# The first product of the last two blocks by seven half-size products per step, with sums of w_in kept in old q/k tiles and three output buffers

## The chip, the cores and the metric

The kernel runs on one core of a Trainium2 chip. The time is the device time of one execution, in microseconds (us); 204.36 is the median of three runs of the kernel before (204.35 to 204.37). One more execution was taken by the profiler. Engines are named as the profile does: PE multiplies matrices (PEld loads its weights, beside it), DVE and ACT work on vectors, POOL and SP issue transfers. SBUF is the working memory of 128 partitions, PSUM the memory of eight banks that PE writes into; a bank holds 128 x 512 fp32 numbers.

## The reference

An attention layer is followed by a two-layer network without bias.

```python
scores = scale * (q @ k.T) + bias            # 4 batches, 8 heads, 768 tokens, head width 64
scores = where(is_global | is_local, scores, -1e9)   # 8 global keys, 96 local keys
a = softmax(scores)
x = (a @ v) as [3072 tokens, 512]
h = x @ w_in                                 # [3072, 2048]   the "first product"
r = maximum(h, 0)
g = r * r
out = g @ w_out                              # [3072, 512]    the "second product"
```

All inputs and the output are fp32; the kernel multiplies in bf16 and accumulates in fp32.

## The kernel before

**Attention** runs over 24 tiles of 128 tokens (j = 0 to 23; six per batch). For each, q, k and v are loaded by POOL's queue (L267, L270), converted to bf16 on the way, into a ring of tiles `qk_ring` (L197); the first tile's q and k come as fp32 into two tiles called plain. q and k are transposed on PE for the first six tiles (words tr and T) and by a DMA on SP's queue from then on (T, L487). Scores (sc), exp on ACT, a multiplication by a mask (mul), the product with v (pv) and the division by the sum (norm) give x, which is transposed into xT, on PE for the first eight tiles, then by a DMA on SP's queue (xT, L795).

**The network** works on 12 blocks of 256 tokens, two tiles each, and splits the hidden width of 2048 into 8 steps of 256. A step of the first product (`emit_s1`, L816 and on, matmul in L826) has 8 matmuls: two halves c of the hidden columns by four parts of the 512 inputs, each with weights of 128x128 from w_in and 256 moving columns of xT. They fill one whole PSUM bank, the tile hT. ACT takes the relu out of it into hr, fp32 (L849), and ACT or DVE squares hr into the bf16 tile hs (L865, L867).

**The second product** of block 0 is plain (L1104). For blocks 1 to 11 it is done by `seven` (L913 and on): the matrices are cut into 2 by 2 parts, and seven products p1 to p7 of half size take the place of eight. Sums of the parts of hs are made by DVE (hsum, L932; words sum), sums of w_out once (w_sum; words wsum), PE adds up the products in two half-filled banks x and y (L975), copies of partial results (part, L390) are taken on ACT or DVE, and `fin` adds these to later products into the output tile o (L1051), of which there are four (NO = 4). SP stores it (L1073).

**Order.** `Plan.run` (L38) emits the operations in the order of the list ORDER (L54 on, 1106 words), which is written into the kernel. A word names an operation, its block or tile and its step: s1.10.3 is step 3 of the first product of block 10, s2.9.p6.1 the second half of product p6 of block 9, @A or @V the engine. Each engine works through its own instructions in the order in which the list has them. The list lets first products run ahead of second ones: before s2.9.p1 there stand s1.10.0 and s1.10.3. PSUM's eight banks are two for `acc` and six, tag "g", for everything else. The waits between engines are put in by the framework, from the tiles that instructions read and write.

Of the kernel before, what the change touches and what calls it, by code (L numbers as in the profile page):

```python
# [54 lines left out]
tr.0.0 T.0.0@A ld.k.1 tr.1.0 ld.q.1 tr.1.1 ld.v.0 bias.0.0 ld.k.2 T.1.1@V tr.0.1 T.1.0@A T.0.1@V sc.0.0 bias.1.0  # L55
sc.1.0 exp.0.1.0 tr.1.2 exp.0.0.0 ld.q.2 exp.1.1.0 bias.1.1 pv.0.0 norm.0.0 exp.1.0.0 ld.q.3 sc.1.1 ld.v.1 T.1.2@A
exp.1.1.1 tr.0.2 gk.1 tr.0.3 T.0.2@V pv.0.1 ld.k.3 exp.1.0.1 bias.2.0 sc.2.0 norm.0.1 pv.1.0 ld.v.2 tr.1.3 norm.1.0
T.0.3@A exp.2.1.0 pv.1.1 exp.2.0.0 T.1.3@V ld.win.0.1 ld.win.0.0 norm.1.1 trx.0 gv.1 ld.win.6.0 xT.0@V bias.2.1 sc.2.1
exp.2.0.1 gk.2 pv.2.0 norm.2.0 exp.2.1.1 trx.1 sc.3.0 sc.3.1 xT.1@V pv.2.1 ld.v.3 exp.3.0.0 exp.3.0.1 E0.0 s1.0.0
exp.3.1.0 s1.0.0#2 s1.0.0#3 s1.0.0#4 ld.win.3.0 s1.0.6 norm.2.1 mul.3.0.0 gv.2 ld.k.4 mul.3.1.0 trx.2 mul.3.0.1  # L60
exp.3.1.1 ld.q.4 mul.3.1.1 pv.3.0 pv.3.1 norm.3.0 norm.3.1 relu.0.0 xT.2@A relu.0.6 ld.win.4.0 s1.0.3 s1.0.3#2 gk.3
sq.0.0@A ones.6 trx.3 tr.1.4 T.1.4@A relu.0.3 ld.win.1.0 tr.0.4 xT.3@V sq.0.6@A s1.1.0 T.0.4@V s1.1.6 ld.q.5 ld.k.5
relu.1.0 s1.1.4 sq.0.3@V sq.1.0@V relu.1.6 ld.win.2.1 ld.win.2.0 gv.3 s1.0.1 sq.1.6@V relu.1.4 s1.0.1#2 sc.4.0
sq.1.4@A relu.0.1 tr.0.5 ld.wout.0 exp.4.0.0 s1.1.3 sq.0.1@V sc.4.1 T.0.5@A s1.0.4 mul.4.0.0 exp.4.1.0 ld.win.5.0 E0.1
ld.v.4 s1.0.2 relu.1.3 sq.1.3@A exp.4.1.1 gk.4 s1.1.2 ld.win.7.0 mul.4.1.0 s2.0.0.0 tr.1.5 relu.1.2 s2.0.0.1 exp.4.0.1
s1.0.2#2 s1.0.2#3 sq.1.2@V ld.v.5 T.1.5@A mul.4.0.1 s1.0.2#4 relu.0.4 ld.wout.2 s1.0.5 ld.wout.1 relu.0.2 sq.0.4@V
pv.4.0 s1.1.7 sq.0.2@A mul.4.1.1 norm.4.0 relu.0.5 relu.1.7 pv.4.1 sc.5.0 norm.4.1 sc.5.1 ld.wout.5 exp.5.0.0 sq.0.5@V
s1.1.5 sq.1.7@A gv.4 mul.5.0.0 exp.5.1.0 exp.5.1.1 s1.0.7 exp.5.0.1 ld.wout.3 relu.1.5 mul.5.1.0 trx.4 xT.4@V
mul.5.0.1 s2.0.1.0 mul.5.1.1 pv.5.0 ld.wout.4 norm.5.0 relu.0.7 s1.1.1 ld.wout.7 pv.5.1 norm.5.1 s2.0.1.1 s2.0.2.1
s2.0.2.0 s2.0.3.0 sq.1.5@V trx.5 s2.0.4.0 s2.0.5.0 s2.0.3.1 s2.0.4.1 wsum.0.0 relu.1.1 ld.wout.6 load.6 load.7 xT.5@V  # L70
sq.1.1@V s2.0.5.1 sq.0.7@A s1.2.0 relu.2.0 sq.2.0@A wsum.0.1 wsum.2.0 s2.0.6.0 sum.1.0 sum.1.1 s2.0.7.0 s1.2.3
relu.2.3 wsum.2.1 gate.8 o.0.0@A wsum.1.0 s2.0.6.1 s2.0.7.1 s1.2.6 s2.1.p1.0 T.6 relu.2.6 T.7 s1.2.7 sq.2.3@A sq.2.6@A
s1.2.5 load.8 s2.1.p1.1 sum.1.3 part.1.p1@A s1.2.4 wsum.1.1 relu.2.5 o.0.1@A s2.1.p6.0 relu.2.7 s1.2.2 st.0.1 sq.2.5@A
st.0.0 s2.1.p2.0 wsum.3.0 relu.2.2 s2.1.p2.1 s2.1.p6.1 sq.2.7@A o.1.p2 sum.1.2 relu.2.4 sc.6.0 part.1.p6@A s2.1.p5.0
exp.6.0.0 sq.2.4@V wsum.3.1 s2.1.p5.1 exp.6.1.0 sc.7.0 mul.6.0.0 sc.7.1 s2.1.p7.0 exp.7.0.0 T.8 s2.1.p7.1 gate.9
sq.2.2@A mul.6.1.0 exp.7.1.1 part.1.p7@V s1.2.1 exp.7.1.0 mul.7.0.0 pv.6.0 mul.7.1.1 o.1.p5 exp.7.0.1 norm.6.0 pv.6.1
relu.2.1 mul.7.1.0 mul.7.0.1 s2.1.p4.0 s2.1.p4.1 sq.2.1@A o.1.p4@A s2.1.p3.0 s2.1.p3.1 norm.6.1 load.9 st.1.1 pv.7.1
pv.7.0 o.1.p3 s2.2.p1.0 st.1.0 norm.7.0 trx.6 norm.7.1 s2.2.p1.1 s2.2.p2.0 xT.6@A trx.7 T.9 gk.7 sum.2.0 s2.2.p2.1
xT.7@V sc.8.0 sc.8.1 s1.3.0 s1.3.3 gate.10 sum.2.1 exp.8.0.0 exp.8.1.0 s1.3.7 part.2.p1@A relu.3.0 load.10 exp.8.0.1
gv.7 mul.8.0.0 sum.2.2 sq.3.0@A s1.3.2 exp.8.1.1 mul.8.0.1 s2.2.p6.0 mul.8.1.0 relu.3.7 s2.2.p6.1 relu.3.2 mul.8.1.1  # L80
load.11 sq.3.7@V o.2.p2 pv.8.1 pv.8.0 relu.3.3 s1.3.5 part.2.p6@A norm.8.0 s2.2.p5.0 s2.2.p7.0 sq.3.3@A sq.3.2@A gk.8
sum.2.3 relu.3.5 s2.2.p5.1 sc.9.0 norm.8.1 gv.8 xT.8 exp.9.1.0 mul.9.1.0 sc.9.1 T.10 load.12 sq.3.5@V exp.9.0.0
exp.9.1.1 mul.9.0.0 exp.9.0.1 s2.2.p7.1 s1.3.1 part.2.p7@V mul.9.1.1 s1.3.6 o.2.p5 relu.3.1 relu.3.6 s1.3.4 sq.3.1@A
pv.9.0 mul.9.0.1 s2.2.p4.0 norm.9.0 pv.9.1 norm.9.1 gk.9 s2.2.p4.1 relu.3.4 sq.3.4@A o.2.p4@A s2.2.p3.0 s2.2.p3.1
sq.3.6@A xT.9 s2.3.p1.0 load.13 o.2.p3 s2.3.p1.1 sum.3.0 s2.3.p2.0 part.3.p1@A T.11 sum.3.1 s2.3.p2.1 sum.3.2 sc.10.0
exp.10.1.0 sc.10.1 s2.3.p6.0 s2.3.p6.1 o.3.p2 exp.10.0.0 gv.9 mul.10.1.0 s2.3.p5.0 s2.3.p5.1 part.3.p6@V exp.10.0.1
mul.10.0.0 exp.10.1.1 s2.3.p7.0 mul.10.0.1 load.14 gk.10 mul.10.1.1 s2.3.p7.1 part.3.p7@A pv.10.0 pv.10.1 s1.4.0
norm.10.0 s1.4.7 norm.10.1 relu.4.0 sc.11.0 sc.11.1 s1.4.4 T.12 relu.4.7 s1.4.3 sq.4.0@V exp.11.0.0 o.3.p5 exp.11.1.1
gv.10 mul.11.0.0 exp.11.1.0 s1.4.2 sq.4.7@V exp.11.0.1 load.15 mul.11.1.0 pv.11.0 relu.4.4 mul.11.1.1 mul.11.0.1
relu.4.3 sc.12.0 sq.4.4@A sq.4.3@V s1.4.5 xT.10 st.2.0 relu.4.2 norm.11.0 exp.12.1.0 pv.11.1 s1.4.6 relu.4.5  # L90
exp.12.0.0 s1.4.1 sq.4.2@V mul.12.1.0 sq.4.5@A s2.3.p4.0 norm.11.1 mul.12.0.0 s2.3.p4.1 pv.12.0 xT.11 relu.4.6
relu.4.1 sum.3.3 sq.4.6@A sq.4.1@V T.13 s2.3.p3.0 o.3.p4@A st.2.1 sum.4.0 s2.3.p3.1 o.3.p3 pv.12.1 sum.4.1 sum.4.2
s2.4.p1.0 s2.4.p1.1 s2.4.p2.0 s2.4.p2.1 part.4.p1@A s2.4.p6.0 s2.4.p6.1 part.4.p6@A o.4.p2 s2.4.p5.0 s2.4.p5.1
s2.4.p7.0 s2.4.p7.1 norm.12.0 norm.12.1 load.16 sc.13.0 sc.13.1 s1.5.0 exp.13.1.0 xT.12 T.14 mul.13.1.0 exp.13.1.1
T.15 exp.13.0.0 sum.4.3 s1.5.3 relu.5.0 part.4.p7@A s1.5.5 mul.13.0.0 mul.13.1.1 exp.13.0.1 sq.5.0@V s2.4.p4.0 pv.13.0
s1.5.1 mul.13.0.1 pv.13.1 relu.5.5 sq.5.5@V s1.5.6 relu.5.3 relu.5.1 norm.13.0 norm.13.1 sq.5.1@A xT.13 sq.5.3@V
s1.5.2 s2.4.p4.1 s1.5.4 relu.5.6 o.4.p5 s1.5.7 s2.4.p3.0 s2.4.p3.1 relu.5.2 sq.5.6@A o.4.p4@V st.3.1 gv.13 gk.13
load.18 sq.5.2@V relu.5.4 relu.5.7 sq.5.4@V sc.14.0 sq.5.7@A o.4.p3 sc.14.1 exp.14.0.0 s2.5.p1.0 s2.5.p1.1 s2.5.p2.0
s2.5.p2.1 sum.5.0 exp.14.1.0 st.3.0 T.16 load.17 part.5.p1@A sum.5.1 exp.14.1.1 mul.14.0.0 mul.14.1.0 mul.14.1.1
s2.5.p6.0 s2.5.p6.1 sum.5.2 pv.14.0 exp.14.0.1 s1.6.1 s1.6.0 norm.14.0 part.5.p6@A kl.14 relu.6.0 mul.14.0.1 o.5.p2  # L100
kl.15 relu.6.1 s2.5.p7.0 pv.14.1 s2.5.p7.1 norm.14.1 sq.6.0@A s2.5.p5.0 part.5.p7@A xT.14 sc.15.0 sc.15.1 s2.5.p5.1
s1.6.4 s1.6.3 exp.15.0.0 sum.5.3 exp.15.1.0 s2.5.p4.0 mul.15.0.0 exp.15.0.1 gv.14 sq.6.1@V s1.6.2 s2.5.p4.1 exp.15.1.1
mul.15.0.1 mul.15.1.1 relu.6.3 mul.15.1.0 o.5.p5 st.4.0 load.19 sq.6.3@A relu.6.4 pv.15.0 s2.5.p3.0 norm.15.0 relu.6.2
pv.15.1 o.5.p4@A norm.15.1 sc.16.1 sq.6.2@V sc.16.0 xT.15 s1.6.7 s2.5.p3.1 sq.6.4@A exp.16.1.0 exp.16.0.0 mul.16.1.0
exp.16.0.1 gv.15 mul.16.0.0 T.17 s1.6.5 exp.16.1.1 relu.6.7 s1.6.6 relu.6.6 o.5.p3 s2.6.p1.0 mul.16.0.1 st.4.1
sq.6.7@A relu.6.5 pv.16.0 mul.16.1.1 sq.6.6@V pv.16.1 s2.6.p2.0 s1.7.0 sq.6.5@V sum.6.0 T.18 load.21 st.5.1 gk.16
s1.7.5 relu.7.0 relu.7.5 s2.6.p2.1 s2.6.p1.1 s1.7.1 norm.16.0 norm.16.1 xT.16 part.6.p1@A sum.6.1 sc.17.0 sc.17.1
gv.16 sq.7.0@A sum.6.3 s2.6.p6.0 s2.6.p6.1 o.6.p2 sq.7.5@A exp.17.1.0 s1.7.3 s2.6.p5.0 sum.6.2 s2.6.p5.1 relu.7.1
load.20 mul.17.1.0 exp.17.0.0 mul.17.0.0 pv.17.0 part.6.p6@A s2.6.p7.0 s1.7.2 s2.6.p7.1 sq.7.1@V exp.17.0.1 relu.7.3
# [1087 lines left out]
```

## Time and profile before

| what | value |
|---|---|
| median of 3 runs | 204.36 us |
| the profiled execution, its own time | 204.49 us |
| its span, first to last instruction | 202.7 us |
| mean granted TensorE clock | 0.998 |
| first product, 736 matmuls of 128x256 (L826) | 90.2 us busy |
| relu on ACT, 96 (L849) | 56.0 us busy, 605 ns each |
| square on DVE, 43 (L867); on ACT, 53 (L865) | 29.5 us; 33.2 us |
| adds of `fin` on DVE, 128x256, 32 (L1051) | 13.4 us busy, 418 ns each |
| PE's longest waits | 1.2 us for the zeros of its warm-up (L333), 0.4 us for an add of `fin` (L975) |

A profile's page has the busy time of each engine and its share of the span, the span cut in 40 slices, the chain of work that ended last, and the groups of instructions by line. In a group's row, x736 is the number of instructions; behind the bar stand the busy time, the mean length of one in ns, and the idle time of the engine just before them with what ended most of it (<- DVE o L1051 means: an instruction of DVE that writes tile o in line 1051). A row of the timeline has the start in us from the span's start, the length of the whole run of like instructions, and in brackets the wait before it.

### The profile page before, as it was taken

The page shows a single profiled execution, that of the slowest core. Times are in us where ns is not written, and L with a number is a line of the kernel's source. Part 1 is how long each engine was busy: PE and PEld are TensorE (multiplying, and loading weights), DVE is VectorE, ACT ScalarE, POOL GpSimd, SP SyncE. Part 2 cuts the span into 40 slices and gives each one's busy share as a digit, 9 for nine tenths or more (in the row PEclk, how much of TensorE's full clock was granted, in tenths as well). Part 3 has the DMA queues.
Part 4 walks back from the last instruction along what each step waited for, and adds up shares of the span by engine and source line. Part 5 has one row for each costly group of instructions (what it writes and reads, how often), then busy time and mean ns, then how long its engine had stood idle before and what let it go on. Part 6 is the DMA issues. An engine that isn't in the chain of part 4 may idle for free.

```text
span 202.7 us, 5686 instructions
## 1 busy us (share of the span) xinstructions
PE 196.9 (97%) x2272; PEld 166.7 (82%) x2272; DVE 148.4 (73%) x404; ACT 146.1 (72%) x289; POOL 75.4 (37%) x93
## 2 busy tenths in 40 slices
PE   7899999999999999999999999999999999999993
PEld 3668878678889888888988988989988888988883
DVE  8289567882897777885888679679669887717843
ACT  6778899448959865964886987696597677848520
POOL 8999776623339425705059004550130000000000
PEclk9999999999999999999999999999999999999999
DMA  8999999999599999996999956999595323031022
GB/s 126 153 173 179 180 184 205 192 147 182 136 175 139 155 130 121 193 179 91 118 235 137 160 118 145 129 160 204 107 143 105 100 78 29 12 118 55 0 110 102
DMA packets 113965, 27.38 MB, mean 135 GB/s; under 512 B 105490, under 2 KB 111122, under 8 KB 113938
## 3 DMA queue, kind: packets, MB, share of 16 engines
q0 software_dynamic: 80256, 13.37, 89.0%
q1 hardware_dynamic: 33682, 13.64, 33.4%
q8 instruction: 18, 0.29, 0.6%
q14 instruction: 9, 0.07, 0.1%
HBM read 27.26 MB, written 6.29 MB: 166 GB/s over the span
## 4 chain that ended last, share of the span: by engine, by line
PE 88%; POOL 6%; DMA 3%; DVE 0%; issue 0%; POOLq 0%
PE hT L826 41%; PE acc L975 34%; PE sc L550 5%; PE po L703 5%; PE acc L1104 3%; DMA qk<-in_q_dram 3%; POOL qk L267 3%; POOL v L267 2%; POOL win L267 1%; PE tr L463 0%; PE trx L771 0%; DVE o L1051 0%; POOL pbi L327 0%; POOLq L327 0%; POOLq L1178 0%
## 5 line engine op out<-in xcount | busy, mean ns | idle before, releaser
L826 PE MATMUL hT<-xT,win 128*128 128x256 bf16 (+1 forms) x800 | 93.8, 268 | 0.0
L826 PEld LDWEIGHTS <-win 128*128 128x128 bf16 x800 | 74.0, 98 | 9.8
L849 ACT ACTIVATE hr<-hT 128x512 f32<-128x512 f32 x96 | 56.0, 605 | 20.8 <-PE hT L826 17.4
L616 ACT ACTIVATE esc<-sc 128x512 bf16<-128x512 f32 x78 | 42.5, 606 | 5.9 <-PE sc L550 5.3
L270 POOL DMA_DIRECT2D qk<-in_q_dram x18 | 16.2, 902 | 66.9 <-DMA qkT<-qk 51.3
L867 DVE TENSOR_TENSOR hs<-hr 128x512 bf16<-128x512 f32 x43 | 29.5, 685 | 15.7 <-ACT hr L849 15.5
L975 PEld LDWEIGHTS <-hsum 128*128 128x128 bf16 x360 | 33.5, 98 | 5.0 <-issue 0.6
L641 DVE TENSOR_TENSOR at<-esc,E 128x512 bf16<-128x512 bf16 x78 | 30.6, 417 | 6.7 <-ACT esc L616 6.3
L975 PE MATMUL acc<-wsum,hsum 128*128 128x256 bf16 x264 | 34.3, 273 | 0.0
L865 ACT ACTIVATE hs<-hr 128x512 bf16<-128x512 f32 x53 | 33.2, 634 | 0.7
L975 PEld LDWEIGHTS <-hs 128*128 128x128 bf16 x264 | 25.0, 98 | 2.9
L975 PE MATMUL acc<-wout,hs 128*128 128x256 bf16 x176 | 23.0, 273 | 0.0
L1051 DVE TENSOR_TENSOR o<-acc,part 128x256 f32<-128x256 f32 (+2 forms) x34 | 14.0, 411 | 10.7 <-PE acc L975 9.3
L734 DVE TENSOR_TENSOR x<-po,rs 128x256 bf16<-128x256 f32 x48 | 20.4, 424 | 1.7
L390 ACT COPY part<-acc 128x256 f32<-128x256 f32 x24 | 9.0, 374 | 15.0 <-PE acc L975 14.6
L703 PE MATMUL po<-v,at 128*128 128x65 bf16 x352 | 17.8, 194 | 0.4 <-DVE v L751 0.3
L703 PEld LDWEIGHTS <-at 128*128 128x128 bf16 x352 | 15.8, 98 | 2.2 <-issue 0.4
L270 POOL DMA_DIRECT2D v<-in_v_dram x18 | 16.4, 911 | 1.3 <-DMA wout<-in_moe_w_out_dram 1.3
L270 POOL DMA_DIRECT2D qk<-in_k_dram x18 | 16.2, 898 | 0.6 <-DMA wout<-in_moe_w_out_dram 0.6
L932 DVE TENSOR_TENSOR hsum<-hs 128x1024 bf16<-128x1024 bf16 (+1 forms) x24 | 15.4, 641 | 1.3 <-ACT hs L865 1.0
L733 DVE RECIPROCAL rs<-po 128x4 f32<-128x4 f32 x48 | 8.6, 179 | 8.7 <-PE po L703 8.2
L550 PEld LDWEIGHTS <-qkT 64*128 64x128 bf16 x312 | 9.5, 94 | 4.6 <-issue 4.0
(62 smaller groups left out, 182.2 us busy)
## 6 DMA issues: line engine op xcount, KB each, us to landing
out_dram<-o SPq DMA_DIRECT2D x22, 256.0 KB, 2.6
v<-in_v_dram POOLq DMA_DIRECT2D x24, 128.0 KB, 5.6
qk<-in_k_dram POOLq DMA_DIRECT2D x23, 128.0 KB, 5.4
qk<-in_q_dram POOLq DMA_DIRECT2D x23, 128.0 KB, 4.8
wout<-in_moe_w_out_dram POOLq DMA_DIRECT2D x8, 256.0 KB, 9.2
win<-in_moe_w_in_dram POOLq DMA_DIRECT2D x6, 256.0 KB, 7.3
win<-in_moe_w_in_dram POOLq DMA_DIRECT2D x4, 128.0 KB, 6.3
out_dram<-o SPq DMA_DIRECT2D x3, 128.0 KB, 1.7
```

The lines of the kernel that those rows point to most:

```text
L270: nc.gpsimd.dma_start(out=dst, in_=src)
L550: nc.tensor.matmul(out=tiles["sc", j, odd, g][:, at, :], lhsT=left[j - 1][half, pair, :] if kt else qkT[j % NKT][half, 1, pair, :], rhs=qk ...
L616: nc.scalar.activation(out=esc, in_=tiles.pop(("sc", j, odd, g)).rearrange("p a c -> p (a c)"), func=Act.Exp, scale=scale,)
L641: nc.vector.tensor_mul(at, tiles.pop(("esc", j, odd, g)), bias)
L703: nc.tensor.matmul(out=po[:, hi, :], lhsT=tiles["at", j, odd, g][:, at * P : (at + 1) * P], rhs=v_sb[kj][:, h, :], start=(i == 0), stop=(i ...
L734: nc.vector.tensor_tensor(out=x[:, 4 * hf : 4 * hf + 4, :], in0=po[:, :, :D], in1=rs.to_broadcast([P, 4, D]), op=Alu.mult,)
L826: nc.tensor.matmul(out=hT[:, c, cols], lhsT=w_in_sb[s][:, kt, c * P : (c + 1) * P], rhs=tiles["xT", blk][:, kt, cols], start=(kt == 0), st ...
L849: nc.scalar.activation(hr, tiles.pop(("hT", blk, s)), Act.Relu)
L865: nc.scalar.activation(hs, hr, Act.Square)
L867: nc.vector.tensor_mul(hs, hr, hr)
L932: nc.vector.tensor_tensor(out=t[:, i, h], in0=t[:, a, h] if isinstance(a, int) else half_a(blk, *a)[:, h], in1=t[:, b, h] if isinstance(b, ...
L975: nc.tensor.matmul(out=tiles["acc", blk, bank][:, cols], lhsT=left_[:, s], rhs=right_[:, cols], start=first and s == 0, stop=s == NSTEP - ...
```

## The change

Blocks 10 and 11 (SEVEN1) take the first product by the same seven products as the second. w_in is cut by halves of the 512 inputs (kh) and of a step's 256 columns (c), xT by halves of the inputs and by its two token tiles.

- `wisum`: eight DVE operations (128x1024, bf16) make four sums of the parts of w_in, for steps 0 to 3 and 4 to 7. They stay in the memory of the first six `qk_ring` tiles and of the two plain tiles, which attention no longer reads then. w_in becomes one tile for that, `w_in_all`.
- `xs`: per block, four DVE operations (128x256, bf16) make the sums of parts of xT.
- `seven1`: per step, seven products of two matmuls each (128x128 weights, 128 moving columns) go into three quarters of the bank hT, in the order p1, p2, p6, p5, p7, p3, p4; p1, p6, p7 and p4 are added up in quarter 0. p1, p6 and p7 are copied out on ACT or DVE (hp), p2, p5 and p3 added to copies by DVE into hr, p4 copied to hr (words ha).
- The relu goes into the square, which in these blocks is one DVE operation, maximum with 0 times hr.
- In the other blocks the relu may run on DVE too; 19 of 80 do.
- Three o tiles in place of four.
- The whole list ORDER is written anew, with 1314 words in place of 1106, over the whole length of the kernel: the loads on POOL's queue come in another order (w_in.1, .2 and .7 before k and q of tile 4), and so do the products, transposes and stores.

The core of the diff (ORDER left out but for some lines of the new one; the bookkeeping of users cut):

```diff
-    w_in_sb = [const([P, KM, 2 * P], BF16, f"win_{s}") for s in range(NSTEP)]
+    w_in_all = const([P, NSTEP, KM, 2 * P], BF16, "win")
+    w_in_sb = [w_in_all[:, s] for s in range(NSTEP)]
...
-    NLATE, NO = 2, 4
+    NLATE, NO = 2, 3
...
+    NXS, NHP, NHR = 1, 2, 2
...
+    homes = [qk_ring[j].rearrange("p n c -> p (n c)") for j in range(NFIRST + 2)]
+    homes += [plain[n, 0].bitcast(BF16) for n in range(2)]
...
+            def emit_wi(e, i=i, a=a, b=b, op=op, h=h, g=g):
+                nc.vector.tensor_tensor(
+                    out=wi_sum[i][g],
+                    in0=wi_sum[a][g] if isinstance(a, int) else wi_part(h, *a),
+                    in1=wi_sum[b][g] if isinstance(b, int) else wi_part(h, *b),
+                    op=op,
+                )
...
+                    nc.vector.tensor_tensor(out=t[:, i], in0=part(a), in1=part(b), op=Alu.subtract)
...
+        seq = [
+            ("p1", 0, (0, 0), (0, 0)), ("p2", 1, (1, 0), (1, 0)), ("p6", 0, 1, 1),
+            ("p5", 2, 0, 0), ("p7", 0, 2, 2), ("p3", 2, 3, (1, 1)), ("p4", 0, (1, 1), 3),
+        ]
+        for name, qr, a, b in seq:
+            def emit_p(e, name=name, qr=qr, a=a, b=b):
+                if name == "p1":
+                    tiles["hT", blk, s] = ps_g.tile([P, 4, P], FP32, name="hT", tag="g")
+                hT = tiles["hT", blk, s]
+                for kt in range(2):
+                    nc.tensor.matmul(
+                        out=hT[:, qr, :],
+                        lhsT=(wi_sum[a][s // 4][:, s % 4] if isinstance(a, int) else wi_part(s, *a))[:, kt],
+                        rhs=tiles["xs", blk][:, b, kt] if isinstance(b, int)
+                        else tiles["xT", blk][:, 2 * b[0] + kt, b[1] * P : (b[1] + 1) * P],
+                        start=name == "p1" and kt == 0,
+                        stop=kt == 1,
+                        skip_group_check=True,
+                    )
+            deps = [last_on.get(qr), first, xT_op[2 * blk], xT_op[2 * blk + 1]]
...
+                    c = work.tile([P, P], FP32, name="hpart", tag="hp_" + name, bufs=NHP)
+                    any_copy(e, c, tiles["hT", blk, s][:, 0, :])
...
+                        tiles["hr", blk, s] = work.tile([P, 2, 2 * P], FP32, name="hr", tag="hr", bufs=NHR)
+                    dst = tiles["hr", blk, s][:, c_, t_ * P : (t_ + 1) * P]
+                    src = tiles["hT", blk, s][:, q_, :]
+                    if other is None:
+                        any_copy(e, dst, src)
+                    else:
+                        nc.vector.tensor_tensor(out=dst, in0=src, in1=tiles["hp", blk, s, other], op=Alu.add)
...
+            if e == "ACT":
+                nc.scalar.activation(hr, hT, Act.Relu)
+            else:
+                nc.vector.tensor_scalar_max(hr, hT, 0.0)
...
+            if blk in SEVEN1:
+                nc.vector.scalar_tensor_tensor(out=hs, in0=hr, scalar=0.0, in1=hr, op0=Alu.max, op1=Alu.mult)
```

Some lines of the new ORDER, from block 10 (xs, s1 with its product, hp and ha are the new words; two or three steps are interleaved):

```
ha.10.4.p5 hp.10.6.p1@A ha.10.3.p2 s1.10.4.p3 s1.10.6.p2 s1.10.6.p5 ha.10.3.p5 sum.9.0 hp.10.7.p1@A sum.9.1 s1.10.6.p6
s1.10.3.p3 part.8.p7@A ha.10.4.p3 xT.23 ha.10.3.p4@A s1.10.4.p4 ha.10.4.p4@A s1.10.7.p5 s1.10.7.p6 s2.8.p4.0 s2.8.p4.1
```

More of the change, by code (lines that the diff above doesn't have):

```diff
@@ L54 @@
 ORDER = """
[L55 to L109, printed above, removed]
@@ L135 @@
[L135 to L139 removed]
+tr.0.0 ld.q.1 T.0.0@V tr.1.0 T.1.0@A ld.k.1 ld.v.1 tr.0.1 bias.0.0 sc.0.0 tr.1.1 T.0.1@V T.1.1@V bias.1.0 sc.1.0
@@ L140 @@
+s2.11.p7.1 sum.11.3 s2.11.p5.1 o.10.p4@A st.10.1 part.11.p7@V s2.11.p4.0 s2.11.p4.1 sum.11.3#2 o.11.p5 st.11.1
+o.11.p4@V st.11.1#2 s2.11.p3.0 s2.11.p3.1 s2.11.p3.0#2 s2.11.p3.1#2 o.11.p3 st.11.0#2 o.11.p3#2 st.11.0#3
 """
@@ L175 @@
     NSTEP = KF // 2
+    SEVEN1 = set(range(10, 12))
     NBLK = NT // 2
@@ L413 @@
     qk_users = [[] for _ in qk_ring]
+    plain_users = [[], []]
     xT_op = {}
@@ L482 @@
             parts.append(c)
-            if not fp:
-                qk_users[slot(j)].append(tr)
+            (plain_users[n] if fp else qk_users[slot(j)]).append(tr)
         if j >= JQK:
@@ new lines @@
+    tiles["old", 6], tiles["old", 7] = [plain_users[0]], [plain_users[1]]
+    for g in range(2 if SEVEN1 else 0):
+        h = slice(4 * g, 4 * g + 4)
+        for i, (a, b, op) in enumerate([
+            ((0, 1), (1, 1), Alu.add), (0, (0, 0), Alu.subtract),
+            ((0, 0), (0, 1), Alu.subtract), ((1, 0), 1, Alu.subtract),
+        ]):
+            def emit_wi(e, i=i, a=a, b=b, op=op, h=h, g=g):
[5 more added lines that the diff above has]
+                )
+            wisum[g, i] = plan.op(
+                ("wisum", g, i), vec(0.62), emit_wi,
+                deps=[land["win", s, c] for s in range(4 * g, 4 * g + 4) for c in range(2 if s in TWO else 1)]
+                + [wisum[g, x] for x in (a, b) if isinstance(x, int)]
+                + [u for us in tiles["old", 2 * i + g] for u in us],
+                key=20.0,
+            )
@@ new lines, in seven1, with emit_xs, part, emit_c @@
+    def seven1(blk, s, n, users):
+        if s == 0:
+            xs_users = tiles["xs_users", blk] = []
+            xsum[blk] = {}
+            for i, (a, b) in enumerate([((0, 1), (0, 0)), ((1, 1), 0), ((1, 1), (0, 1)), ((1, 0), 1)]):
+                def emit_xs(e, i=i, a=a, b=b):
+                    if i == 0:
+                        tiles["xs", blk] = work.tile([P, 4, 2, P], BF16, name="xs", tag="xs", bufs=NXS)
+                    t = tiles["xs", blk]
+                    def part(x):
+                        return t[:, x] if isinstance(x, int) else tiles["xT", blk][:, 2 * x[0] : 2 * x[0] + 2, x[1] * P : (x[1] + 1) * P]
+                    nc.vector.tensor_tensor(out=t[:, i], in0=part(a), in1=part(b), op=Alu.subtract)
+                o = plan.op(
+                    ("xs", blk, i), vec(0.21), emit_xs,
+                    deps=[xT_op[2 * blk], xT_op[2 * blk + 1]] + [xsum[blk][x] for x in (a, b) if isinstance(x, int)]
+                    + ([xsum[blk][0]] if i == 2 else []),
+                    key=n - 1.0, takes=("xs", NXS, [xs_users]) if i == 0 else None,
+                )
+                xsum[blk][i] = o
+                xs_users.append(o)
+                xT_of[blk].append(o)
+        xs_users = tiles["xs_users", blk]
+        rusers = []
+        last_on = {}
+        copied = {}
+        done = []
+        seq = [
+            ("p1", 0, (0, 0), (0, 0)), ("p2", 1, (1, 0), (1, 0)), ("p6", 0, 1, 1),
+            ("p5", 2, 0, 0), ("p7", 0, 2, 2), ("p3", 2, 3, (1, 1)), ("p4", 0, (1, 1), 3),
+        ]
+        first = None
+        for name, qr, a, b in seq:
[12 more added lines that the diff above has]
+                        skip_group_check=True,
+                    )
+            deps = [last_on.get(qr), first, xT_op[2 * blk], xT_op[2 * blk + 1]]
+            deps += [wisum[s // 4, a]] if isinstance(a, int) else [land["win", s, c] for c in range(2 if s in TWO else 1)]
+            if isinstance(b, int):
+                deps.append(xsum[blk][b])
+            o = plan.op(
+                ("s1", blk, s, name), {"PE": 0.11}, emit_p, deps=deps, key=float(n),
+                takes=(*G, [users]) if name == "p1" else None,
+            )
+            first = first or o
+            users.append(o)
+            xT_of[blk].append(o)
+            if isinstance(b, int):
+                xs_users.append(o)
+            last_on[qr] = o
+            if name in ("p1", "p6", "p7"):
+                cu = []
+                def emit_c(e, name=name):
+                    c = work.tile([P, P], FP32, name="hpart", tag="hp_" + name, bufs=NHP)
+                    any_copy(e, c, tiles["hT", blk, s][:, 0, :])
+                    tiles["hp", blk, s, name] = c
+                c = plan.op(
+                    ("hp", blk, s, name), {"ACT": 0.21, "DVE": 0.2}, emit_c, deps=[o], key=n + 0.1,
+                    takes=("hp_" + name, NHP, [cu]),
+                )
+                cu.append(c)
+                copied[name] = c, cu
+                users.append(c)
+                last_on[0] = c
+            pairs = {"p2": [("p2", 1, 0, 0, "p1")], "p7": [("p5", 2, 1, 1, "p7")], "p3": [("p3", 2, 0, 1, "p6")],
+                     "p4": [("p4", 0, 1, 0, None)]}.get(name, [])
+            for nm, q_, c_, t_, other in pairs:
+                def emit_a(e, q_=q_, c_=c_, t_=t_, other=other, opens=not done):
+                    if opens:
+                        tiles["hr", blk, s] = work.tile([P, 2, 2 * P], FP32, name="hr", tag="hr", bufs=NHR)
[5 more added lines that the diff above has]
+                        nc.vector.tensor_tensor(out=dst, in0=src, in1=tiles["hp", blk, s, other], op=Alu.add)
+                d = plan.op(
+                    ("ha", blk, s, nm), {"ACT": 0.21, "DVE": 0.2} if other is None else vec(0.2), emit_a,
+                    deps=[last_on[q_], copied[other][0] if other else None] + done[:1], key=n + 0.4,
+                    takes=("hr", NHR, [rusers]) if not done else None,
+                )
+                users.append(d)
+                rusers.append(d)
+                done.append(d)
+                last_on[q_] = d
+                if other:
+                    copied[other][1].append(d)
+        return done, rusers
@@ L844 @@
             xT_of[blk].append(a)
-        s1_ops[blk, s] = a
+        if blk not in SEVEN1:
+            s1_ops[blk, s] = a
         def emit_relu(e, blk=blk, s=s):
-            hr = work.tile([P, 2, 2 * P], FP32, name="hr", tag="hr")
-            nc.scalar.activation(hr, tiles.pop(("hT", blk, s)), Act.Relu)
-            tiles["hr", blk, s] = hr
-        rusers = []
-        r = plan.op(("relu", blk, s), {"ACT": 0.48}, emit_relu, deps=[a], key=n + 0.5, takes=("hr", 2, [rusers]))
-        users.append(r)
-        rusers.append(r)
+            hr = work.tile([P, 2, 2 * P], FP32, name="hr", tag="hr", bufs=NHR)
+            hT = tiles.pop(("hT", blk, s))
+            if e == "ACT":
+                nc.scalar.activation(hr, hT, Act.Relu)
+            else:
+                nc.vector.tensor_scalar_max(hr, hT, 0.0)
+            tiles["hr", blk, s] = hr
+        if blk not in SEVEN1:
+            rusers = []
+            r = plan.op(("relu", blk, s), {"ACT": 0.48, "DVE": 0.61}, emit_relu, deps=[a], key=n + 0.5, takes=("hr", NHR, [rusers]))
+            users.append(r)
+            rusers.append(r)
+            r = [r]
         if s == 0:
@@ L869 @@
         d = plan.op(
-            ("sq", blk, s), {"ACT": 0.52, "DVE": 0.61}, emit_sq,
-            deps=[r] + [square[blk, 0][0] for _ in range(s > 0)], key=n + 1.0,
+            ("sq", blk, s), vec(0.61) if blk in SEVEN1 else {"ACT": 0.52, "DVE": 0.61}, emit_sq,
+            deps=r + [square[blk, 0][0] for _ in range(s > 0)], key=n + 1.0,
             takes=("hs", NHB, [husers]) if s == 0 else None,
```

147 lines of the change are left out of this document (115 added, 32 removed).

## The prediction

> **What bounds the kernel now.** All times are microseconds of the profiled execution, which took 204.49 with a span of 202.7; the median of the runs is 204.36, 0.13 less. First the page: busy time per engine, then the chain that ended last.
>
> ```profile
> PE 196.9 (97%) x2272; PEld 166.7 (82%) x2272; DVE 148.4 (73%) x404; ACT 146.1 (72%) x289; POOL 75.4 (37%) x93
> ...
> PE 88%; POOL 6%; DMA 3%; DVE 0%; issue 0%; POOLq 0%
> ```
>
> TensorE (PE) is busy 97% of the span and is 88% of the chain; the rest is the loads at the start. A kernel like this gets shorter only by less PE work, and longer by any wait put into PE's queue. The change touches the last two blocks, so next the windows of the end (columns: window, its length, busy time of PE, PEld, DVE, ACT, POOL with counts, granted clock, DMA share, GB/s).
>
> ```profile
> 150.00:160.00 10.00, 10.00 (x127) 8.83 (x126) 8.90 (x26) 8.07 (x16) 0.00 (x0) 1.00 0.90 135
> ...
> 170.00:180.00 10.00, 10.00 (x106) 9.01 (x104) 5.19 (x13) 5.85 (x12) 0.00 (x0) 1.00 0.30 54
> 180.00:190.00 10.00, 10.00 (x94) 8.96 (x93) 6.98 (x14) 8.56 (x16) 0.00 (x0) 1.00 0.14 54
> 190.00:202.70 12.70, 9.61 (x95) 8.47 (x92) 5.94 (x15) 1.70 (x5) 0.00 (x0) 0.97 0.24 85
> ```
>
> PE has no idle time until the last products; DVE has 3 to 5 us free of every ten, ACT 1.4 to 11. That is the room into which the change puts its additions. Groups and timeline give the prices:
>
> ```profile
> L826 PE MATMUL hT<-xT,win 128*128 128x256 bf16 x736 | 90.2, 273 | 0.0
> L867 DVE TENSOR_TENSOR hs<-hr 128x512 bf16<-128x512 f32 x43 | 29.5, 685 | 15.7 <-ACT hr L849 15.5
> L390 ACT COPY part<-acc 128x256 f32<-128x256 f32 x24 | 9.0, 374 | 15.0 <-PE acc L975 14.6
> L1051 DVE TENSOR_TENSOR o<-acc,part 128x64 f32<-128x64 f32 x1 | 0.2, 224 | 0.5 <-PE acc L975 0.5
> ```
>
> ```profile
> 19.99 0.39 PE L463 MATMUL tr<-ident,qk 128*128 128x128 bf16 x4
> 24.94 1.04 PE L826 MATMUL hT<-xT,win 128*128 128x256 bf16 x8
> ```
>
> **PE work.** Eight 256-column products take 1.04, the last of them 0.27: (1.04 - 0.27)/7 = 0.110, and over longer stretches 0.109 each. Four 128-column ones, each with its own weights, take 0.39 with 0.22 for the last: (0.39 - 0.22)/3 = 0.056. A step of the first product was 8 x 0.109 = 0.872 and becomes 14 x 0.056 = 0.784; 16 steps save **1.41**.
>
> By a sentence of the Trainium skill, "TensorE: Matmul & The Clock Gate", section "Back-to-back issue gap", a sustained stream of weight load and 128-column product runs at about 81 ns each, which speaks against this change: the term would be an estimated 16 x (14 x 0.081 - 0.872) = +4.2 instead of -1.41. The row above has 0.056 with a new weight load for each, though only in fours.
>
> **DVE and ACT work.** Per step ACT loses a 605 ns relu and often a 634 ns square, and gets four 128-column copies. Copies of 256 columns take 374 and follow one another at about 0.26; half the columns I put at 0.265 and 0.15. DVE gets three 128-column adds. The 256-column add takes 418, the 64-column 224: on a line, 0.285; back to back 0.20. It also gets every square, 0.685 (0.60 back to back). So DVE has 3 x 0.20 + 0.60 = 1.20 a step, ACT 0.60, beside 0.784 of PE. Counted from the start of sc.23.0 to s2.11.p1.1, the last wait for a square, PE has 34.5 of work in the new order and DVE 35.1: DVE alone would hold PE back 0.35 to 0.9.
>
> The eight sums of w_in (128x1024, as the 685 ns hsum row, 0.60 back to back, 4.8 in all) and the relus moved to DVE fall between steps 2 and 9 of the blocks, where DVE's work comes to 86 to 90% of PE's: I cost them at nothing; the cover is that tenth, and without it at most these 4.8 are paid. The xs sums (0.2 each) of block 11 are in the 35.1; those of block 10 lie ahead of it, under PE. Three o buffers instead of four: the first tile of block 11 waits for the first store of block 10; the 256 KB stores land 2.6 after issue, so the buffer is free about 4.0 after the last square and wanted at 4.8, cost nothing, 0.7 to spare. The loads on POOL's queue come in another order (w_in earlier, later q and k tiles later); added up by landing times, the data of the first steps are short by 9.4 to 9.5 both before and after; 0, within 0.4 either way. The DMA transposes on SP keep 0.5 or more of slack by their median landing (4.6 and 3.7), which their slowest (7.9 and 6.3) would use up; 0, at worst 3.
>
> **The waits, which decide.** The plan's dependencies treat the three quarters of the tile hT as separate. They lie in one PSUM bank, and in the built program every product into that bank waits for the ACT and DVE instructions issued earlier that read any quarter of it; these also wait for each other. Before has one place of the same form: the closing 64-column products behind the add that reads the other 192 columns of their bank.
>
> ```profile
> 199.25 0.36 DVE L1051 TENSOR_TENSOR o<-acc,part 128x192 f32<-128x192 f32 x1 [0.24 <-PE acc L975]
> ...
> 199.66 0.39 PE L975 MATMUL acc<-wout,hsum 128*128 128x64 bf16 x8 [0.45 <-DVE o L1051]
> ```
>
> The add reads other columns, yet the products start only at 199.66, 0.05 after it ends: PE stood 0.45.
>
> The Trainium skill, "PSUM — Partial Sum Buffer", section "PSUM bank collisions raise a hardware error", says to guard by bank and quadrant of partitions, not by address, two readers included; the 0.45 agrees, and no row here shows two readers.
>
> So a step is a chain. A pair of products is done 0.275 after its start; each hand-over is about 0.035. p1 0.28, its copy 0.30, p6 0.32, copy 0.30, p7 0.32, copy 0.30, add of p5 0.31, p3 0.32, add 0.32, p4 0.32, copy 0.30, square 0.72; with the add of p2 between two of the copies 0.2 more: 4.3. The order written out keeps two steps in flight (hp and hr have two buffers each): 16 x 4.3/2 = 34, as long as PE's own 34.5. Nothing is left for an engine that is busy with something else when a link is due, and PE issues in order: a product that waits holds all behind it, the second products of block 9 and 10 included.
>
> I walked the written order by these prices from sc.23.0, each instruction starting when its engine and what it waits for are done. PE stands:
> - at p3 or p4 behind an add or copy in the same bank: 1.28 at step 4 of block 10 (its add is queued on DVE behind two sums of block 9), 0.59 and 0.47 at steps 1 and 6, twice 0.09; in block 11 three of 0.5, then 0.45, 0.31, 0.25 and 0.08: 5.1 in all;
> - at p6 or p7: 0.38, 0.8, 0.5 and three below 0.2: 2.0;
> - elsewhere (the first tile's bank, second products behind an add, the last squares): 1.1.
>
> Together **8.2**; DVE's own excess of 0.35 to 0.9 lies inside it. Behind the last square, the last product of block 11 waits for a copy now on DVE: **+0.2**.
>
> Sum: 204.49 - 1.41 + 8.2 + 0.2 = 211.5; against the median 0.13 less, **211.3**. No trace of before shows such a chain, so its price is bounded from 0.35 (no wait but DVE's load) to 16 x 4.3 - 34.5 = 34 (no overlap); I take the walk, since its links come from near rows. A tenth on each link is 0.4 a step or about 3 in the sum, so this case's own range is 208.5 to 214.
>
> **Rivals.**
> - The waits do not bite: the order overlaps them, PE is held only by DVE's load. 204.49 - 1.41 + (0.35 to 0.9) + 0.2 = 203.6 to 204.2, faster. For it: the free time of DVE and ACT in the windows. Against it: the 0.45 above. It decides if a product may start while another quarter is read. 0.14, of which 0.03 lies within 0.2% (0.4 us, about what a measurement of this kernel can tell from no change).
> - Half bites: copies and adds of 128 columns at their back-to-back prices (0.15, 0.20) shorten a step by some 0.9, to 3.4, and 2 to 4.5 of stalls are left: 205 to 208. For it: both engines' queues often hold several of them. 0.20, of which 0.01 within 0.2%.
> - 128-column products in pairs cost 0.08, not 0.056. PE then has 16 x 14 x 0.025 = 5.6 more: 204.5 + 4.2 = 208.7 with no stall, up to 216 with all. Against it: the 0.39 row. The skill's rule above is this one. 0.05.
> - The change saves nothing since its operands are late: a transpose of a tile at the slow end, or w_in sums that hold up the middle; 3 to 5 on top of the forecast, 214 to 217. Before has slack there. 0.06.
>
> **Chances.** Forecast 0.55, and so faster 0.11, the same 0.04, slower 0.85. The range must leave out at most 0.2: from 204.6 (the no-wait case, 0.14, lies below) to 214 (0.06 above).
>
> **What would show it.** In the new trace PE has idle time from about 156 on where before had none: some 8 us in the windows, named as waits of hT products on the adds into hr (DVE) and on the copies (ACT), most before the sixth and seventh product of a step. The 14 products of an undisturbed step start 0.056 apart; the copies take 0.27, the adds 0.28. DVE is busy 80% or more there. I am wrong if PE's windows stay at 10.00, if the pairs stand near 0.08, or if PE waits before block 10 at all.

## The result, and the profile after

The changed kernel takes 215.11 us (median of six runs, 213.59 to 217.09), the kernel before 204.36 beside it (204.15 to 204.93): a ratio of 1.050, 95% interval 1.046 to 1.054. The run of 217.09 counts as slow, and the ratio is of the other five. The forecast was 211.3, with a range up to 214.0: the side was right, the size was 3.8 us short. The profiled execution took 215.4, its span is 213.6. These are the same two lines of its page, busy time by engine and the chain that ended last:

```profile
PE 199.3 (93%) x2368; PEld 167.4 (78%) x2368; DVE 175.7 (82%) x483; ACT 143.7 (67%) x322; POOL 75.1 (35%) x93
...
PE 69%; DMA 11%; DVE 9%; POOL 6%; ACT 2%; issue 2%; SPq 0%; DVEq 0%; ACTq 0%; POOLq 0%
```

The span grew by 10.9 and PE's share of the chain fell from 88% to 69%; DMA (11%) and DVE (9%) took over. Where PE stands is seen in the windows (columns as in the prediction: window, its length, busy time of PE, PEld, DVE, ACT, POOL, clock, DMA share, GB/s):

```profile
70.00:80.00 10.00, 8.91 (x105) 7.76 (x103) 7.70 (x19) 5.97 (x12) 2.43 (x3) 1.00 1.60 144
...
140.00:150.00 10.00, 9.16 (x129) 7.79 (x128) 9.09 (x29) 7.61 (x16) 2.63 (x3) 1.00 1.38 133
...
160.00:170.00 10.00, 9.02 (x122) 7.83 (x121) 8.26 (x26) 7.47 (x24) 0.00 (x0) 1.00 0.34 68
170.00:180.00 10.00, 8.32 (x109) 7.58 (x108) 7.59 (x22) 4.42 (x18) 0.00 (x0) 1.00 0.14 42
180.00:190.00 10.00, 8.98 (x108) 7.62 (x106) 8.67 (x27) 4.74 (x21) 0.00 (x0) 1.00 0.15 54
190.00:200.00 10.00, 8.33 (x89) 6.90 (x87) 7.98 (x22) 4.06 (x18) 0.00 (x0) 1.00 0.14 54
```

From 160 on, where the seven-product steps begin, PE is 10% to 17% idle, and neither DVE nor ACT is full at the same time: nobody is at its limit, all wait for one another. Two earlier windows have a hole of about 1 us each, far away from the changed blocks. PE's waits by cause (engine and line that waited, what it waited for: us in total, times, longest) name both:

```profile
PE hT L912 <- DVE hr L963: 4.3, 8, 1.1
PE sc L576 <- DMA qkT<-qk: 1.9, 2, 1.1
...
PE hT L912 <- ACT hpart L416: 1.1, 3, 0.4
```

The first and the third are products of a step behind the adds and copies out of its bank; the second are two attention tiles whose transposed q and k came late.

"Idle" below is finer than in the windows: the start of each product less the start of the one before and less its back-to-back price (0.216, 0.109, 0.056 and 0.029 for 512, 256, 128 and 64 or 65 columns), summed. It is given for three stretches, the start, the middle, and the part with the seven-product steps:

| kernel | PE work | idle 0 to 30 | idle 30 to 160 | idle from 160 | median of runs |
|---|---|---|---|---|---|
| before | 188.0 | 5.7 | 3.9 | 1.1 | 204.4 to 204.8 |
| changed | 186.6 | 6.5 | 6.1 | 9.8 | 215.11 |
| e1, plain product in the new order | 188.0 | 6.4 | 6.0 | 1.5 | 207.65 |
| e2, p3 and p4 together | 186.6 | 6.6 | 5.5 | 6.4 | 211.15 |
| e3, before with three buffers | 188.0 | 5.5 | 12.4 | 1.4 | 213.22 |
| e4, two transposes sooner | 186.6 | 5.8 | 7.7 | 9.9 | 214.55 |
| e5, two banks a step | 186.6 | 5.7 | 6.5 | 1.0 | 207.06 |
| e6, the order of e5, one bank | 186.6 | 5.8 | 6.4 | 12.7 | 219.49 |
| e7, one bank, planned for it | 186.6 | 5.5 | 7.0 | 2.5 | 208.34 |
| e8, two banks, early order of before | 186.0 | 6.3 | 14.4 | 1.7 | 216.08 |
| e9, as e8, another order | 186.0 | 6.3 | 17.2 | 1.6 | 217.44 |
| e10, two banks, transfers in before's order | 186.0 | 5.8 | 15.8 | 2.1 | 215.57 |
| e11, as e10, another last third | 186.0 | 6.7 | 15.0 | 2.5 | 215.61 |

The traces of e8 to e11 have no record of three of the 2368 products: their work is 186.6 like that of the others, and 0.6 of their idle time is these three.

For the changed kernel the columns give the whole difference: work -1.4, start +0.8, middle +2.2, steps +8.7, and 0.6 more between the last product and the end; 204.5 + 10.9 = 215.4.

### The profile page after: what moved, and what is told of

It reads as the page before. It is cut to its first block, busy times and chain, and to the rows that moved or that the text cites. A ratio compares the mean times of both kernels' runs of the same rounds, so it can differ in the third digit from the quotient of the medians.

```text
span 213.6 us, 6021 instructions
## 1 busy us (share of the span) xinstructions
PE 199.3 (93%) x2368; PEld 167.4 (78%) x2368; DVE 175.7 (82%) x483; ACT 143.7 (67%) x322; POOL 75.1 (35%) x93
## 4 chain that ended last, share of the span: by engine, by line
PE 69%; DMA 11%; DVE 9%; POOL 6%; ACT 2%; issue 2%; SPq 0%; DVEq 0%; ACTq 0%; POOLq 0%
PE hT L992 29%; PE acc L1152 23%; DMA qkT<-qk 8%; PE sc L576 5%; PE hT L912 4%; PE po L729 4%; PE acc L1281 3%; DVE hr L963 3%; DMA win<-in_moe_w_in_dram 3%; POOL qk L293 3%; DVE hs L1040 2%; DVE hsum L1109 2%; POOL v L293 2%; POOL win L293 1%; DVE o L1228 1%
## 5 line engine op out<-in xcount | busy, mean ns | idle before, releaser
L992 PE MATMUL hT<-xT,win 128*128 128x256 bf16 (+1 forms) x672 | 78.3, 268 | 0.8 <-DMA win<-in_moe_w_in_dram 0.7
L992 PEld LDWEIGHTS <-win 128*128 128x128 bf16 x672 | 61.4, 98 | 9.0 <-DMA win<-in_moe_w_in_dram 1.2
L1020 ACT ACTIVATE hr<-hT 128x512 f32<-128x512 f32 x61 | 35.8, 600 | 11.8 <-PE hT L992 8.3
L1152 PEld LDWEIGHTS <-hsum 128*128 128x128 bf16 x360 | 32.6, 98 | 4.8 <-issue 0.4
L1152 PE MATMUL acc<-wsum,hsum 128*128 128x256 bf16 x264 | 35.4, 273 | 0.3 <-DVE o L1228 0.2
L416 ACT COPY hpart<-hT 128x128 f32<-128x128 f32 x46 | 11.1, 271 | 12.1 <-DVE hr L963 7.4
L963 DVE TENSOR_TENSOR hr<-hT,hpart 128x128 f32<-128x128 f32 x48 | 12.4, 286 | 6.7 <-PE hT L912 4.0
L1044 DVE TENSOR_TENSOR hs<-hr 128x512 bf16<-128x512 f32 x25 | 16.8, 682 | 0.7 <-ACT hr L1020 0.6
L1022 DVE TENSOR_SCALAR hr<-hT 128x512 f32<-128x512 f32 x19 | 13.0, 685 | 4.1 <-PE hT L992 1.9
L576 PE MATMUL sc<-qkT 64*128 64x128 bf16 x192 | 13.1, 219 | 2.5 <-DMA qkT<-qk 1.9
```

Of the source, the lines that this page charges most:

```text
L576: nc.tensor.matmul(out=tiles["sc", j, odd, g][:, at, :], lhsT=left[j - 1][half, pair, :] if kt else qkT[j % NKT][half, 1, pair, :], rhs=qk ...
L963: nc.vector.tensor_tensor(out=dst, in0=src, in1=tiles["hp", blk, s, other], op=Alu.add)
L992: nc.tensor.matmul(out=hT[:, c, cols], lhsT=w_in_sb[s][:, kt, c * P : (c + 1) * P], rhs=tiles["xT", blk][:, kt, cols], start=(kt == 0), st ...
L1020: nc.scalar.activation(hr, hT, Act.Relu)
L1044: nc.vector.tensor_mul(hs, hr, hr)
L1152: nc.tensor.matmul(out=tiles["acc", blk, bank][:, cols], lhsT=left_[:, s], rhs=right_[:, cols], start=first and s == 0, stop=s == NSTEP - ...
```

## The experiments

Medians are compared with runs of the kernel before on the same chip (204.6 to 204.8).

**e1: the new order without the new product.** SEVEN1 is empty; each step is eight plain products at the place of p6, the relu on ACT where the second copy was. The sums of w_in and of xT are left out.

```diff
-    SEVEN1 = set(range(10, 12))
+    SEVEN1 = set()
...
-s1.10.0.p1 ... s1.10.0.p6 ... hp.10.0.p6@A ... sq.10.0
+s1.10.0 ... relu.10.0@A ... sq.10.0@V
```

> The new order and three output buffers, but blocks 10 and 11 take the first product by the eight plain products, the relu on ACT where the second copy stood, the square on DVE where it stood; the sums of w_in and xT are left out. Theory A (the stalls behind reads of the same PSUM bank belong to the seven-product steps): PE works 1.4 more, but the 8 us of stalls from 156 us on go; what is left against before is the late q/k transposes (2.2) and the start (0.8): about 207.0 (206 to 208). Rival B (the new order itself starves PE at the end, whatever the product): 212 or more, with PE idle by 5 us or more after 156 us. Rival C (DVE is overloaded at the end): as A, since its load falls by 0.6 a step.

Measured: 207.65, ratio 1.014 (1.010 to 1.017). The idle time from 160 on is gone (1.5), that of the middle is not. So about 7.5 us of the loss belong to the seven-product steps, though they have less work, and 3 us to the new order before them. Rival B is out.

**e2: fewer products behind a read of their bank.** Some 17 words move within their step; engines and work stay.

```diff
-s1.10.4.p3 ... ha.10.4.p3 ... ha.10.3.p4@A s1.10.4.p4 ha.10.4.p4@A
+s1.10.4.p3 s1.10.4.p4 ... ha.10.4.p3 ... ha.10.3.p4@A ha.10.4.p4@A
```

> The changed kernel with the same instructions on the same engines; only the places in the order of p3 and p4 of 13 steps (one moved next to the other, and the adds that read them behind both) and of one p7 (ahead of an add of its bank) are changed, so that fewer products stand behind a read of another quarter of their bank. Theory A: the stalls of 1.3, 0.8, 0.7 us and a few of 0.3 to 0.5 go, some 3 us of the 8: about 212 (211 to 213). Rival C (DVE or ACT hold PE back by their load, the wait shown is only where it surfaces): no gain, 214.5 to 215.5, stalls of the same sum at other places.

Measured: 211.15, ratio 1.031 (1.029 to 1.034): 4 us less than the changed kernel, more than the 3 expected, by the places of some words alone. The load of DVE is the same, so it was not what held PE in these 4 us. Of the idle time from 160 on, 6.4 us are left.

**e3: three buffers alone.** `NO = 2, 4` becomes 3 in the kernel before.

> The kernel before with three output buffers in place of four, nothing else. Theory A: no add waits for a store, 204.4 (204.2 to 204.6). Rival: the first add of a block waits for the store of the block before, 204.8 to 206.

Measured: 213.22, ratio 1.041 (1.039 to 1.044). Both were wrong by far. The timeline of DVE (start, length, what, wait before it) shows why:

```profile
86.59 0.42 DVE L1051 TENSOR_TENSOR o<-acc,part 128x256 f32<-128x256 f32 x1 [5.57 <-DMA out_dram<-o]
```

In the old order a store stands on SP's queue behind a transpose and is issued at 81.32, after the add that now needs its buffer has come up on DVE (81.02). It lands 5.25 later, where the prediction counted with 2.6 for a store. The add waits 5.57 and everything DVE has behind it waits too; PE stands 3.8 for that, and a second add waits 3.04 at 110.29. The windows show one more loss, in the granted clock (the third column from the end):

```profile
80.00:90.00 10.00, 5.57 (x64) 4.14 (x63) 4.05 (x12) 4.76 (x10) 4.36 (x5) 0.84 1.84 147
90.00:100.00 10.00, 10.00 (x89) 8.44 (x88) 7.36 (x17) 5.10 (x11) 2.27 (x3) 0.82 0.33 70
```

From 86.9 to 93.6 it is 0.50, and eight products of 256 columns take 1.89 there instead of 1.04; that is some 2 of the 8.6 us, an estimate from the starts of the products in that stretch. In the new order, planned for three, e1 has two such waits of 0.6 and less on DVE, the changed kernel one of 0.3, and none of PE's waits is named for a store. "Costs nothing" was right for the changed kernel with its new order; in the old order it was not.

**e4: two transposes sooner.**

```diff
-xT.8 gv.8 s2.2.p5.0 T.10
+T.10 xT.8 gv.8 s2.2.p5.0
...
-xT.17 ... load.22 ... xT.18 ... T.20
+xT.17 T.20 ... load.22 ... xT.18
```

> The changed kernel, with only the DMA transposes of tiles 10 and 20 issued sooner on SP's queue: tile 10's ahead of the xT of tile 8, tile 20's right behind the xT of tile 17 instead of behind the xT of tile 18. Theory A: the two waits of 1.1 and 0.8 us for qkT (2.2 us lost with their aftermath) go: about 213.0 (212.5 to 213.7). Rival (the transfers are slow by the loads beside them, so an earlier issue lands no earlier, or delays another transpose): 214.5 to 215.5.

Measured: 214.55, ratio 1.050 (1.044 to 1.055), no gain that can be told. The two waits are gone: tile 20's transpose was issued 2.9 sooner and landed 4.7 sooner, tile 10's was issued 1.2 sooner and landed 1.3 sooner, still 8.62 after its issue though it now stood ahead of the xT of tile 8. But PE waits for later ones on the queue:

```profile
145.23 0.23 PE L579 MATMUL sc<-qkT 64*128 64x128 bf16 x2 [0.81 <-DMA qkT<-qk]
...
148.89 1.03 PE L995 MATMUL hT<-xT,win 128*128 128x256 bf16 x8 [1.82 <-DMA xT<-x]
```

The time is the rival's, by its second half: an earlier issue did land earlier, and other transposes came late. The wait of 1.82 is not the edit's alone, since e1, which issues the transposes as the changed kernel does, waits 1.1 for the same xT.

**e5 and e6: two banks, and the same order with one.** In e5 p2, p5 and p3 go to a bank of their own. The order from the middle on is planned anew for that. e6 is that order and that code, with the three quarters in one tile again.

```diff
-                if name == "p1":
-                    tiles["hT", blk, s] = ps_g.tile([P, 4, P], FP32, name="hT", tag="g")
-                hT = tiles["hT", blk, s]
+                key = ("hT", blk, s, qr > 0)
+                opens = key not in tiles
+                if opens:
+                    tiles[key] = ps_g.tile([P, 2, P], FP32, name="hU" if qr else "hT", tag="g")
+                hT = tiles[key]
...
```

> The same seven products, copies, adds and squares as the changed kernel, but a step's results lie in two PSUM banks: quarter 0 (p1, p6, p7, p4) in one, p2 and p5 + p3 in another, so that a read of p2, p5 or p3 no longer stands in the way of p6, p7 and p4. The order from the middle of the kernel on is planned anew for that, with the transposes issued earlier against their use; the start is the changed kernel's. Theory A (the stalls are the price of one bank): PE hardly waits after 156 us, the saved 1.4 stay, less 0.8 for the start: about 204 (203 to 206). Rival C (the load of DVE, 1.2 a step, or the chain of a step holds PE back, in whatever banks): 208 or more.

> The order and the instructions of the kernel with two banks a step, but all three quarters of a step in one bank again, as in the changed kernel. Theory A: every product behind a read of another quarter waits again, 9 to 12 us more than with two banks, 213 to 217. Rival C: within 1 us of the kernel with two banks.

Measured: 207.06 (ratio 1.012, 1.009 to 1.015) and 219.49 (1.072, 1.068 to 1.076), 12.4 us apart. Both times lie above theory A's ranges, by 1.1 and 2.5, and e5's below rival C's; the distance between the two is near the 9 to 12 of theory A, where rival C had put it within 1. The windows, first of e5, then of e6:

```profile
170.00:180.00 10.00, 9.94 (x125) 9.02 (x123) 9.97 (x33) 5.85 (x26) 0.00 (x0) 1.00 0.28 93
180.00:190.00 10.00, 10.00 (x130) 9.37 (x128) 9.97 (x29) 5.59 (x23) 0.00 (x0) 1.00 0.13 52
```

```profile
170.00:180.00 10.00, 7.70 (x104) 6.64 (x101) 7.83 (x24) 5.22 (x20) 0.00 (x0) 1.00 0.15 41
180.00:190.00 10.00, 8.27 (x93) 6.94 (x91) 7.95 (x24) 4.08 (x17) 0.00 (x0) 1.00 0.14 54
```

With two banks PE and DVE are both full, to 99%: DVE's load just fits, as the prediction's 35.1 against 34.5 had it. With one bank both are idle a fifth of the time. PE's waits in e6 are the ones of the changed kernel (`hT` behind `hr` on DVE, 3.3, and behind copies on ACT, 3.3); e5 has none of them. This shows the cause of the idle time in the steps: one bank for all of a step's results. Whether the bank or the tile in it makes the wait, no run tells, since e5 gives p2, p5 and p3 a tile of their own along with the bank. The profiled execution of e5 took 206.3, 1.8 more than that of before: the work saves 1.4, the idle time of the middle is 2.6 higher (transposes again, tile 10's alone 0.7), and the last product is followed by 0.6 more.

**e7: one bank, an order that knows it.** All code of the changed kernel; the order from the middle on is planned with the waits by bank.

> One bank a step as in the changed kernel, the same instructions, with the order from the middle on planned with the waits by bank and with slower transposes in mind. Theory A: the stalls come from an order that did not know of these waits, not from the work: some 2 us of them are left at the end, about 205.5 (204 to 207). Rival C (the load of DVE or the chain of a step): 209 or more.

Measured: 208.34 (ratio 1.017, 1.015 to 1.020). From 160 on 2.5 are left of 9.8. It is 2.8 above what was expected, outside theory A's range and below rival C's, most of it in the middle (7.0 of idle time against 3.9), 1.1 of that the wait for tile 10.

**e8 to e11: two banks and the old start.** e8 and e9 keep the order of before at the start, up to the 150th word (some 28 us, not the 65 that were meant), and plan the rest twice anew; e10 and e11 keep it to the 240th word, and every load and transpose in the order of before.

> Two banks a step as in e5_two_banks, but the order of the kernel before up to about 65 us, loads included, and the middle and the end planned from there; three output buffers and the sums of w_in as in the changed kernel. Theory A: with the start of before (0.8 better) and without the late transpose of tile 10 (0.8), and the 1.4 of saved work kept but for about 0.7 of small waits and a longer close: 204.0 (203.3 to 204.8), so no more than 0.3% to either side of before. Rival (what was lost in the kernel with two banks beside the start lies in the steps themselves): 206 or more.

> As e8_two_banks_old_start, with another planned order of the middle and the end; how much the order alone decides. Theory A: within 0.8 of e8, 203.5 to 205. Rival: as there, 206 or more.

> Two banks a step as in e5_two_banks, with the loads on POOL's queue and the transposes on SP's queue in exactly the order of the kernel before, and the same order of everything up to about 45 us; only stores are issued sooner (three buffers), and the work of the engines is planned anew around it. What e8 and e9 lost between 20 and 50 us came from loads that had been moved; theory A now gives: start and transposes as before, 1.4 of PE work saved, some 1 us of small waits at the end: 204.0 (203.3 to 205.0). Rival (the steps themselves, or the eight sums of w_in on DVE, cost more than that): 206 or more.

> As e10_two_banks_old_dma, with another order of the last third: how much the order alone decides. Theory A: 204.4 (203.5 to 205.5). Rival: as there, 206 or more.

Measured: 216.08, 217.44, 215.57 and 215.61 (ratios 1.057, 1.062, 1.051 and 1.051, each within 0.005). All four expectations missed by 11 to 13 us, and the times lie in the rivals' ranges, but not for the rivals' reason: from 160 on PE is idle 1.6 to 2.5, as hoped, and the loss lies at 30 to 160, where it is idle for 14 to 17. PE's waits, first of e8, then of e10:

```profile
PE po L732 <- DMA v<-in_v_dram: 3.0, 1, 3.0
PE acc L1289 <- DMA wout<-in_moe_w_out_dram: 1.6, 2, 1.4
```

```profile
PE sc L579 <- DMA qkT<-qk: 4.9, 3, 2.4
```

e8 had moved loads, and they came late (e9, with the same start, waits 5.9 for transposes). e10 moved none, only the work around them; with it the transpose of tile 6 is issued at 45.22 instead of 42.73 and lands after 6.5 instead of 4.4, tile 10's after 8.8 instead of 5.5, tile 19's after 8.5 instead of 7.5. The clock adds to it: it is 0.50 for 3.4 us in e8 and e11, for 6.8 in e9 and twice for 3.4 in e10, which by the starts of the products is an estimated 1 to 2.5 of the 14 to 17. Orders found by counting engine work, with one landing time for all transfers, won nothing here, where transfers have half a microsecond to spare. A version that is faster than before was not found; whether two banks a step would be, with transfers as punctual as before's, stays open: an estimate from the columns of e5 is 203.5 to 204 (204.5 - 1.4, and 0.6 at the end).

## Why the prediction was right or wrong

**The price of the products: right.** 16 steps save 1.41 of PE work. In the changed kernel 190 products of the steps follow another directly; the middle one starts 0.056 after it, and 179 of them less than 0.07, each with a new weight load, in stretches of 2 to 24. The rule of the Trainium skill ("TensorE: Matmul & The Clock Gate", section "Back-to-back issue gap"), about 81 ns for each in a stream, is not what this trace shows. The third rival falls with it. (Its 216 "with all" is 217 by its own terms, 208.7 + 8.2 + 0.2.)

**The prices of copies and adds: right.** The copies and adds of 128 columns had been put at 0.265 and 0.285, from other widths of before; the groups after (busy, mean ns, then idle before) have 271 and 286:

```profile
L963 DVE TENSOR_TENSOR hr<-hT,hpart 128x128 f32<-128x128 f32 x48 | 12.4, 286 | 6.7 <-PE hT L912 4.0 <-ACT hpart L416 2.0
L416 ACT COPY hpart<-hT 128x128 f32<-128x128 f32 x46 | 11.1, 271 | 12.1 <-DVE hr L963 7.4 <-PE hT L912 4.6
```

**The waits by bank: right, place by place.** Forecast 8.2 and 0.2 at the end; measured 8.7 more idle time from 160 on. At p3 and p4 PE stands 6.0 (forecast 5.1), at p6 and p7 2.7 (2.0), elsewhere 1.0 (1.1); before's own 1.1 is not taken off here. The longest had been put at 1.28, p4 of step 4 of block 10 behind its add, which is behind two sums. On DVE and then on PE:

```profile
175.34 0.68 DVE L1109 TENSOR_TENSOR hsum<-hs 128x1024 bf16<-128x1024 bf16 x1
176.05 0.69 DVE L1109 TENSOR_TENSOR hsum<-hsum,hs 128x1024 bf16<-128x1024 bf16 x1
176.66 0.48 DVE L963 TENSOR_TENSOR hr<-hT,hpart 128x128 f32<-128x128 f32 x2
```

```profile
177.00 0.27 PE L912 MATMUL hT<-xs,win 128*128 128x128 bf16 x2 [1.14 <-DVE hr L963]
```

The add, of another quarter, starts after the second sum and ends about 176.95; the product starts 0.05 later, 1.30 after it could have. Others: 0.89 (forecast 0.8, p7 of step 2), 0.70 (0.59, p3 of step 1), 0.49 (0.47, step 6). That putting a step's results in one bank, and not DVE's load or the steps' dependencies, is the cause, e2, e5 and e6 show. The rivals that had the waits hidden or halved are out. The first of them leaned on 3 to 5 us of ten free on DVE; the windows give that from 170 on, while from 150 to 170 there is about 1 free.

The Trainium skill's rule ("PSUM — Partial Sum Buffer", section "PSUM bank collisions raise a hardware error") is to guard by bank and quadrant of partitions. The waits of the built program agree with it as far as the bank goes, at a price of 12.4 us between e5 and e6; no run here tells one quadrant from another, or the bank from the tile.

**The transfers: wrong, and this is the step that failed.** The prediction said of the transposes on SP: "0.5 or more of slack by their median landing [...], which their slowest would use up; 0, at worst 3", and of the loads "0, within 0.4". Measured: 2.2 in the middle, which is two waits of 1.25 and 1.0,

```profile
77.09 0.23 PE L576 MATMUL sc<-qkT 64*128 64x128 bf16 x2 [1.09 <-DMA qkT<-qk]
```

```profile
142.93 0.23 PE L576 MATMUL sc<-qkT 64*128 64x128 bf16 x2 [0.84 <-DMA qkT<-qk]
```

and 0.8 at the start. The profiled execution was forecast at 211.5 and took 215.4; the 3.9 between are these 2.2 and 0.8, 0.5 in the steps and 0.4 at the end. The 2.2 belong to the new order: e1 has 2.1 and e2 1.6, though in e1 the waits are for tile 10 (0.5) and for an xT (1.1). The 0.8 may be chance: e2 and e4 to e7 have the same order up to 30 us, and while e2 is idle 6.6 there, the others are 5.5 to 5.8, as before is with 5.7.

The first wait is tile 10's: issued at 68.31, hardly other than in the kernel before (68.70), it landed after 8.7 instead of 5.5, and after 7.9 to 8.4 in e1, e2 and e5 to e7, which have the same order there. Nine loads of three tiles were issued beside it on POOL's queue from 61.35 on, in before from 60.31 on; so more of them were still under way. The second is tile 20's: wanted 6 us sooner in the new order, it was issued 7 us sooner, just behind the loads of tile 22, and took 7.5. That the loads are what slows a transpose is read from these traces; no run took the loads away. A median over all transposes says nothing of one with nine loads beside it. This should have been a term of about 2, with the case of a higher time (0.06 in the prediction) as its upper half; the range then would have reached 217. The prediction had named the sign itself: "I am wrong [...] if PE waits before block 10 at all"; both waits lie before it.

**The end: small, unseen.** The order puts the two last adds behind both last products of the same bank: the span ends 3.4 after the last product's start instead of 2.8.

**No term** was wrong on the sums of w_in: PE is at 10.00 in every window of ten from 30 to 140 but that of tile 10's wait, and the sums lie there.
